# Issuing four kinds of store from GpSimd's queue in a one-core chain of attention and two feed-forward blocks

## The chip, the cores and the metric

The kernel runs on one core of one Trainium2 chip. The metric is device time in microseconds (us) of one execution. Engines are named as in the profile: PE (TensorE; PEld its weight loads), DVE (VectorE), ACT (ScalarE), POOL (GpSimd), SP (SyncE, which here only issues DMAs).

## The reference, cut to what matters

```python
# attention: 4 batches, 8 heads, 576 positions, 64 wide; heads 0-3 local mask, heads 4-7 strided mask
attn = softmax(where(mask, q @ k.T / 8, -1e9)) @ v      # -> x: 2304 tokens x 512
a = x @ w1                                              # 512 -> 1024
b = x @ w2                                              # 512 -> 1024
h = a * b @ w3                                          # 1024 -> 1024
y = h @ w_out                                           # 1024 -> 512
h = y @ w_in                                            # 512 -> 2048
g = h * sigmoid(1.702 * h)
out = g @ w_out2                                        # 2048 -> 512
```

## The kernel before

All products run in float32r with each operand split into a high and a low part; three matmuls (high*low, low*high, high*high) make one product. ACT makes the high part (L221) and DVE the low part (L227). `w3 @ w_out` is folded into one matrix first (L768), so the first block is `y = (a*b) @ wf`. Weights come in as 8-byte raw words; `to_f32` (L236 and L237 on ACT, L238 to L240 on DVE) turns them into float32 before the split.

The kernel has these stages, in order of time. An opening written out by hand (to about 45 us, `tc.manual_schedule`). Then for each of the 4 batches of 576 tokens, in halves of 288 columns: `g1` makes `a` and `b` for one of 8 row blocks m (12 matmuls each, L635), ACT copies `a` out of PSUM (L661) into a tile `abf`, and DVE multiplies `b` into it (L663). For batches 0 and 1 the product `a*b` goes out to DRAM (`abdram`, L667) and comes back later (`back`, L673); for batches 2 and 3 it is split at once into `ab`. `g2` multiplies by the folded matrix in two runs of 12 matmuls (L684); ACT copies the result into `ysb` (L690) and it is stored to `ydram` (L692). In between, `u_conv(0)` to `u_conv(7)` convert the second block's `w_in`, form the sums of a Strassen-like scheme and store them to `widram` (L946); `u_conv(8)` to `u_conv(15)` convert `w_out2` and store its parts to `wodram` (L948). From about 455 us the second block runs: `w_fetch` loads factors back from `widram` (L1006), `wt_fetch` parts from `wodram` (L1042), `quad` and `o_group` multiply (L1071, L1117), and `put` stores the output (L1131).

Tiles come from pools with a fixed number of buffers: `abf` 3, `ysb` 2, PSUM tiles `mm` 4. In the conversion of `w_out2` there are two raw tiles, one for even and one for odd numbers, and one tile `x` in two halves, so `u_conv(i + 2)` writes the half that the store of part i must have read. Parts are fetched back into the even raw tile alone, so part n + 1 is fetched when the low split of part n is done.

The text calls the eight steps `u_conv(8)` to `u_conv(15)` conversions 8 to 15, and the four parts that are split ahead of the second block parts 0 to 3 (their tiles are `w_66`, `w_68`, `w_70` and `w_72` in the listings below). The last half of batch 3 has eight `g1` groups, numbered 1 to 8 here, and four `g2` groups; `ab` of group 8 is needed by the last 3 of the 24 matmuls of the first `g2` group.

The source gives the order of recording (`weave` mixes lists by marks between 0 and 1). Outside the opening, a list scheduler then orders each engine's instructions by modelled durations, so an edit of one queue can change the order on every engine. Each engine works its list in order, and an instruction that waits holds up everything behind it; SP's list of DMA issues too.

Of the kernel before, what the change touches and what calls it, by code (L numbers as in the profile page):

```python
# [39 lines left out]
HB = S // 2  # L40
# [4 lines left out]
CW2 = 1024  # L45
# [4 lines left out]
NU = 8  # L50
# [138 lines left out]
def body(ctx: ExitStack, tc, qk, vv, mask, ql, vl, qs, vs, qmask, w1, w2, w3t, wo, win, wout, out):  # L189
    nc = tc.nc  # L190
# [20 lines left out]
    ydram = dram.tile([KC, P, NT], F32, name="ydram")  # L211
    abdram = dram.tile([4, MC, P, HB], F32, name="abdram")
    widram = dram.tile([NU, P, 7 * 256], F32, name="widram")
    wodram = dram.tile([NU, P, CW2], F32, name="wodram")
# [18 lines left out]
    def to_f32(xf, raw, n):  # L233
        rf, ri, ru = (raw.bitcast(t).rearrange("p (n t) -> p n t", t=2)[:, :n] for t in (F32, I32, U32))
        x = xf.bitcast(I32)
        nc.scalar.activation(xf, rf[:, :, 1], AF.Copy, scale=REBIAS)  # L236
        nc.scalar.activation(ri[:, :, 0], ru[:, :, 0], AF.Copy, scale=LOW)  # L237
        nc.vector.tensor_scalar(x, x, 3, BODY, op0=ALU.logical_shift_left, op1=ALU.bitwise_and)  # L238
        nc.vector.scalar_tensor_tensor(x, ri[:, :, 1], SIGN, x, op0=ALU.bitwise_and, op1=ALU.bitwise_or)  # L239
        nc.vector.tensor_tensor(x, x, ri[:, :, 0], op=ALU.add)  # L240
# [389 lines left out]
    def first(xh, cols, m, which, ps):  # L630
        ws = (w1u, w2u)[which]
        for k in range(KC):
            at = m % 2 * CW + k * P
            for a, c in ORDER:
                nc.tensor.matmul(  # L635
                    ps, ws[a][m // 2][:, at:at + P], xh[c][:, k, cols],
                    start=(k == 0 and (a, c) == ORDER[0]), stop=(k == KC - 1 and (a, c) == ORDER[-1]),
                )
# [5 lines left out]
    def new_ab(hb, m, hold, f):  # L644
        ab = abs_[m // 4][:, m % 4]
        split_ab(ab, f)
        hold[hb, m] = ab

    def g1(b, hb, m, hold, away=None):

        cols = slice(hb * HB, (hb + 1) * HB)
        st = {}

        def one(which):
            if which == 0:
                st[0] = p1.tile([P, HB], F32, tag="abf", name="abf", bufs=3)
            f = st[0]
            ps = mm.tile([P, HB], F32, tag="mm", name="ps")
            first(xt[b], cols, m, which, ps)
            if which == 0:  # L660
                nc.scalar.activation(f, ps, AF.Copy)  # L661
            else:
                nc.vector.tensor_tensor(f, ps, f, op=ALU.mult)  # L663
                if away is None:
                    new_ab(hb, m, hold, f)
                else:
                    nc.sync.dma_start(abdram[away, m], f)  # L667

        return [lambda: one(0), lambda: one(1)]

# [5 lines left out]
    def g2(b, hb, n, hold):  # L676
        st = {}

        def one(half):
            if half == 0:  # L680
                st[0] = mm.tile([P, HB], F32, tag="mm", name="ps")
            for k in range(4 * half, 4 * half + 4):
                for a, c in ORDER:
                    nc.tensor.matmul(  # L684
                        st[0], wfs[a][k][:, n * P:(n + 1) * P], hold[hb, k][:, c],
                        start=(k == 0 and (a, c) == ORDER[0]), stop=(k == MC - 1 and (a, c) == ORDER[-1]),
                    )
            if half == 1:
                ysb = p1.tile([P, HB], F32, tag="ysb", name="ysb", bufs=2)
                nc.scalar.activation(ysb, st[0], AF.Copy)  # L690
                c0 = b * S + hb * HB
                nc.sync.dma_start(ydram[n, :, c0:c0 + HB], ysb)  # L692

        return [lambda: one(0), lambda: one(1)]

# [104 lines left out]
    def half_step(k, i, h):  # L800
# [11 lines left out]
            x, x, 3, BODY, op0=ALU.logical_shift_left, op1=ALU.bitwise_and  # L812
# [108 lines left out]
    def u_load(i):  # L921

        if i >= 2 * NU:
            return
        raw = cv[i % len(cv)].tile([P, CW2], I64, tag="raw", name="raw", bufs=2 if len(cv) == 1 else 1)
        nc.sync.dma_start(raw, win[i] if i < NU else wout[i - NU])
        todo[i] = raw

    def u_conv(i, last=False):
        raw = todo.pop(i)  # L930
        if i < NU:
            x = cv[0].tile([P, 2 * CW2], F32, tag="x", name="x")
        else:
            if i == NU:
                todo["x"] = cv[0].tile([P, 2 * CW2], F32, tag="x", name="x")
            x = todo["x"][:, i % 2 * CW2:(i % 2 + 1) * CW2]
        to_f32(x[:, :CW2], raw, CW2)
        if not last:
            u_load(i + 2)
        if i < NU:  # L940
            a21, a11, a12, a22, s1, s2, s3, s4 = (x[:, n * 256:(n + 1) * 256] for n in range(8))
            nc.vector.tensor_tensor(s1, a21, a22, op=ALU.add)
            nc.vector.tensor_tensor(s2, s1, a11, op=ALU.subtract)
            nc.vector.tensor_tensor(s3, a11, a21, op=ALU.subtract)
            nc.vector.tensor_tensor(s4, a12, s2, op=ALU.subtract)
            nc.sync.dma_start(widram[i], x[:, 256:])  # L946
        else:
            nc.sync.dma_start(wodram[i - NU], x[:, :CW2])  # L948

    def u_convs(lo, hi, ahead=True):  # L950
        return [lambda i=i: u_conv(i, not ahead and i + 2 >= hi) for i in range(lo, hi)]
# [246 lines left out]
```

## Time and profile before

| | before |
|---|---|
| median of 3 runs | 841.48 us (840.9 to 843.92) |
| the profiled execution | 841.14 us |
| its span, first to last instruction | 839.3 us |
| PE busy | 804.8 us (96%) |
| DVE busy | 570.6 us (68%) |
| ACT busy | 424.4 us (51%) |
| POOL busy | 5.8 us (1%) |
| DMA moved | 117.70 MB, mean 140 GB/s |
| mean granted PE clock | 0.998 |

The profiled execution lies 1.8 us above its span and 0.3 us below the median. PE is busy nearly throughout after the first 40 us, so time is lost or won only where PE waits.

### The profile page before, as it was taken

What the parts mean: (1) busy time and instruction counts of PE and PEld (TensorE: products, weight loads), DVE (VectorE), ACT (ScalarE), POOL (GpSimd) and SP (SyncE); (2) the same over time, 40 slices, a digit from 0 to 9 for tenths busy, and PEclk for the clock granted to TensorE, in tenths of its full rate; (3) what the DMA queues carried; (4) which work ended last, traced back from release to release, by engine and by line L of the source; (5) the groups of instructions that cost most, each with busy time, mean ns of one, the idle gap of its engine ahead of it and who ended that gap; (6) DMA issues with size and microseconds to landing.
All of it is one profiled execution on the core that took longest, in us unless ns stands there. A gap on an engine that the chain in (4) does not pass through costs nothing.

```text
span 839.3 us, 15033 instructions
## 1 busy us (share of the span) xinstructions
PE 804.8 (96%) x5882; PEld 731.3 (87%) x5882; DVE 570.6 (68%) x1244; ACT 424.4 (51%) x900; POOL 5.8 (1%) x14
## 2 busy tenths in 40 slices
PE   3798999999999999999989999999999999999998
PEld 2688999977989999999989899988999988999986
DVE  3789595289776787657564988863877863877730
ACT  4788664267664564445443655542445442445330
POOL 2000000000000000000000000000000000000000
PEclk9999999999999999999999999999999999999999
DMA  9588364235676553142875441232221232212011
GB/s 344 210 307 287 108 192 137 80 123 160 241 244 207 197 201 116 51 146 103 296 234 173 143 165 59 86 113 82 87 70 64 89 113 82 89 56 77 1 38 37
DMA packets 40999, 117.70 MB, mean 140 GB/s; under 512 B 4576, under 2 KB 22496, under 8 KB 37600
## 3 DMA queue, kind: packets, MB, share of 16 engines
q1 hardware_dynamic: 40784, 116.70, 40.4%
q8 instruction: 46, 0.75, 0.4%
q14 instruction: 25, 0.20, 0.1%
q10 hardware_dynamic: 144, 0.04, 0.0%
HBM read 91.04 MB, written 25.69 MB: 139 GB/s over the span
## 4 chain that ended last, share of the span: by engine, by line
PE 79%; DMA 6%; DVE 6%; ACT 5%; issue 3%; SPq 0%; ACTq 0%; DVEq 0%
PE acc L1117 24%; PE ps L1071 20%; PE ps L635 19%; PE ps L684 9%; PE acc L768 2%; DMA wodram<-x 2%; PE sc L531 1%; PE pv L589 1%; DMA raw<-in_wout 1%; DMA abf<-abdram 1%; DMA raw<-in_w 1%; ACT xw L236 1%; ACT w L221 1%; DVE x L239 1%; DVE w L227 1%
## 5 line engine op out<-in xcount | busy, mean ns | idle before, releaser
L1117 PE MATMUL acc<-w,w 128*128 128x512 f32 x864 | 209.3, 397 | 0.0
L1117 PEld LDWEIGHTS acc<-w,w 128*128 128x128 f32 x864 | 161.7, 188 | 36.4 <-ACT w L221 0.6
L1071 PE MATMUL ps<-yq,hl 128*128 128x384 f32 x1008 | 184.2, 337 | 1.0 <-DVE hl L227 0.7
L1071 PEld LDWEIGHTS ps<-yq,hl 128*128 128x128 f32 x1008 | 177.7, 188 | 5.4 <-DVE hl L227 1.0
L684 PE MATMUL ps<-ab,w 128*128 128x288 f32 x768 | 111.2, 302 | 4.8 <-ACT abf L661 2.8
L684 PEld LDWEIGHTS ps<-ab,w 128*128 128x128 f32 x768 | 104.9, 191 | 8.5 <-DVE ab L227 3.3
L635 PE MATMUL ps<-xbh,w 128*128 128x288 f32 x512 | 102.6, 295 | 0.0
L635 PE MATMUL ps<-xah,w 128*128 128x288 f32 x512 | 102.1, 295 | 0.0
L635 PEld LDWEIGHTS ps<-xbh,w 128*128 128x128 f32 x512 | 82.1, 188 | 0.0
L635 PEld LDWEIGHTS ps<-xah,w 128*128 128x128 f32 x512 | 82.1, 188 | 0.0
L635 PE MATMUL ps<-xbl,w 128*128 128x288 f32 x256 | 78.6, 308 | 0.8 <-ACT w L221 0.7
L1062 ACT ACTIVATE sg<-c 128x384 f32<-128x384 f32 x48 | 25.0, 524 | 102.9 <-DVE c L1077 102.8
L635 PE MATMUL ps<-xal,w 128*128 128x288 f32 x256 | 76.3, 298 | 0.0
L1077 DVE TENSOR_TENSOR u<-ps,u 128x384 f32<-128x384 f32 x96 | 53.2, 554 | 10.9 <-PE ps L1071 8.9
L227 DVE TENSOR_TENSOR hl<-x,hl 128x1792 fp32r<-128x1792 f32 x24 | 48.6, 2025 | 14.0 <-ACT hl L221 14.0
L663 DVE TENSOR_TENSOR abf<-ps,abf 128x288 f32<-128x288 f32 x64 | 28.9, 453 | 33.4 <-PE ps L635 21.0
L635 PEld LDWEIGHTS ps<-xbl,w 128*128 128x128 f32 x256 | 48.0, 188 | 3.9 <-ACT w L221 0.9
L227 DVE TENSOR_TENSOR w<-gr,w 128x384 fp32r<-128x384 f32 x48 | 26.4, 557 | 33.5 <-ACT w L221 33.5
L221 ACT ACTIVATE ab<-abf 128x288 fp32r<-128x288 f32 x64 | 27.5, 441 | 42.5 <-DVE abf L663 35.7
L635 PEld LDWEIGHTS ps<-xal,w 128*128 128x128 f32 x256 | 48.1, 188 | 0.9 <-issue 0.2
L768 PE MATMUL acc<-w,w 128*128 128x512 f32 x192 | 48.0, 402 | 0.9 <-ACT w L221 0.7
L221 ACT ACTIVATE w<-gr 128x384 fp32r<-128x384 f32 x48 | 24.9, 523 | 40.6 <-PE acc L1117 40.6
(142 smaller groups left out, 1021.2 us busy)
## 6 DMA issues: line engine op xcount, KB each, us to landing
x<-widram SPq DMA_DIRECT2D x24, 896.0 KB, 4.5
raw<-in_win SPq DMA_DIRECT2D x8, 1024.0 KB, 5.6
raw<-in_wout SPq DMA_DIRECT2D x8, 1024.0 KB, 6.7
widram<-x SPq DMA_DIRECT2D x8, 896.0 KB, 5.0
raw<-in_w3t SPq DMA_DIRECT2D x10, 512.0 KB, 4.1
abdram<-abf SPq DMA_DIRECT2D x32, 144.0 KB, 2.1
abf<-abdram SPq DMA_DIRECT2D x32, 144.0 KB, 3.3
ydram<-ysb SPq DMA_DIRECT2D x32, 144.0 KB, 2.4
```

Of the source, the lines that this page charges most:

```text
L221: nc.scalar.activation(hi, src, AF.Copy)
L227: e.tensor_tensor(lo, src, r(hi), op=ALU.subtract)
L236: nc.scalar.activation(xf, rf[:, :, 1], AF.Copy, scale=REBIAS)
L239: nc.vector.scalar_tensor_tensor(x, ri[:, :, 1], SIGN, x, op0=ALU.bitwise_and, op1=ALU.bitwise_or)
L635: nc.tensor.matmul(ps, ws[a][m // 2][:, at:at + P], xh[c][:, k, cols], start=(k == 0 and (a, c) == ORDER[0]), stop=(k == KC - 1 and (a, c) ...
L663: nc.vector.tensor_tensor(f, ps, f, op=ALU.mult)
L684: nc.tensor.matmul(st[0], wfs[a][k][:, n * P:(n + 1) * P], hold[hb, k][:, c], start=(k == 0 and (a, c) == ORDER[0]), stop=(k == MC - 1 and ...
L768: nc.tensor.matmul(acc[f], hl[:, a, f * P:(f + 1) * P], wor[c][g], start=(g == 0 and (a, c) == ORDER[0]), stop=(g == MC - 1 and (a, c) == ...
L1062: nc.scalar.activation(sg, src, AF.Sigmoid, scale=1.702)
L1071: nc.tensor.matmul(ps, w[:, a, f * 256 + kk * P:f * 256 + (kk + 1) * P], yq[:, b, kk, c], start=(kk == 0 and (a, c) == ORDER[0]), stop=(kk ...
L1077: nc.vector.tensor_tensor(dst, x, y, op=ALU.add)
L1117: nc.tensor.matmul(acc[t], g[:, a, t * P:(t + 1) * P], wt[i][:, c, half], start=(i == half == 0 and (a, c) == ORDER[0]), stop=(i == NU - 1 ...
```

## The change

The DMAs of four kinds of store move from SP's queue to POOL's: `a*b` to `abdram` (32 DMAs), `y` to `ydram` (32), the `w_in` factors to `widram` (8) and the `w_out2` parts to `wodram` (8). All loads, and the output's 18 stores, stay on SP.

```diff
@@ g1
                 if away is None:
                     new_ab(hb, m, hold, f)
                 else:
-                    nc.sync.dma_start(abdram[away, m], f)
+                    nc.gpsimd.dma_start(abdram[away, m], f)
@@ g2
                 ysb = p1.tile([P, HB], F32, tag="ysb", name="ysb", bufs=2)
                 nc.scalar.activation(ysb, st[0], AF.Copy)
                 c0 = b * S + hb * HB
-                nc.sync.dma_start(ydram[n, :, c0:c0 + HB], ysb)
+                nc.gpsimd.dma_start(ydram[n, :, c0:c0 + HB], ysb)
@@ u_conv
-            nc.sync.dma_start(widram[i], x[:, 256:])
+            nc.gpsimd.dma_start(widram[i], x[:, 256:])
         else:
-            nc.sync.dma_start(wodram[i - NU], x[:, :CW2])
+            nc.gpsimd.dma_start(wodram[i - NU], x[:, :CW2])
```

The first place is SP's list behind the opening, in the listing's form with - for before and + for now; the rows L749 load raw words of `w1` and `w2`.

```order
 L297 DMA qs<-in_qs 128x1168
-L667 DMA abdram<-abf 128x288 x2
 L309 DMA vst_112<-in_vs 128x1024
 L874 DMA msk<-in_mask 128x512
 L749 DMA raw<-in_w 128x1024 x3
-L667 DMA abdram<-abf 128x288
 L294 DMA ql<-in_ql 128x896
```

The first two stores of `a*b` stood ahead of those loads and are gone from the list.

The second place is DVE's list from conversion 12 on, among the last eight `g1` groups; this is the piece of before.

```order
-L227 TENSOR_TENSOR ab_2621<-abf,ab_2621 128x288
-L663 TENSOR_TENSOR abf<-ps,abf 128x288
-L238 TENSOR_SCALAR x<-x 128x1024
-L227 TENSOR_TENSOR ab_2621<-abf,ab_2621 128x288
-L239 SCALAR_TENSOR_TENSOR x<-raw,x 128x1024
-L240 ISA x<-raw,x 128x2048
-L663 TENSOR_TENSOR abf<-ps,abf 128x288
```

And this is the piece that stands there now.

```order
+L238 TENSOR_SCALAR x<-x 128x1024
+L239 SCALAR_TENSOR_TENSOR x<-raw,x 128x1024
+L227 TENSOR_TENSOR ab_2621<-abf,ab_2621 128x288
+L240 ISA x<-raw,x 128x2048
+L238 TENSOR_SCALAR x<-x 128x1024
+L663 TENSOR_TENSOR abf<-ps,abf 128x288
+L239 SCALAR_TENSOR_TENSOR x<-raw,x 128x1024
```

Before, the product of group 2 (the first L663) stood ahead of conversion 12; now it stands behind all of 12 and the first step of 13.

The third place is ACT's list behind conversion 15, where `ab_2622` are the high splits of groups 6 to 8 and `w_66` and `w_68` those of parts 0 and 1.

```order
 L661 ACTIVATE abf<-ps 128x288
 L221 ACTIVATE w_66<-raw 128x1024
 L221 ACTIVATE ab_2622<-abf 128x288
-L690 ACTIVATE ysb<-ps 128x288
+L661 ACTIVATE abf<-ps 128x288
+L221 ACTIVATE ab_2622<-abf 128x288
+L661 ACTIVATE abf<-ps 128x288
 L221 ACTIVATE w_68<-raw 128x1024
+L221 ACTIVATE ab_2622<-abf 128x288
+L690 ACTIVATE ysb<-ps 128x288
```

Before, the split of group 8 (the first `ab_2622` row) followed part 0 alone; now part 0 stands two groups earlier, behind group 6, and the split of group 8 follows part 1. Inside a conversion the two ACT steps have also changed places: before, L237 (in place on the raw tile) came ahead of L236 (which writes the half of `x`); now L236 comes first.

## Rows read from the trace of the kernel before

**Rows 1.** Busy time by stage: us, each engine's busy us (instructions), clock, DMA share, GB/s.

```profile
90.00:390.00 300.00, 298.37 (x2232) 272.82 (x2232) 209.09 (x601) 164.87 (x437) 0.78 (x2) 1.00 0.48 159
390.00:465.00 75.00, 69.92 (x491) 68.58 (x490) 44.05 (x58) 35.81 (x54) 0.00 (x0) 0.98 0.60 198
```

**Rows 2.** Waits of SP's queue: total us, times, longest us.

```profile
SPq L667 <- DVE abf L663: 72.8, 23, 22.2
```

**Rows 3.** Timeline behind the opening: SP, DVE, ACT, PE; start us, us, instruction, [idle before].

```profile
43.34 1.53 SPq L667 DMA_DIRECT2D abdram<-abf  x2
45.93 3.31 SPq L749 DMA_DIRECT2D raw<-in_w  x3
...
38.38 0.68 DVE L817 CUSTOM_DVE_ANT_0 xw<-raw,xw 128x1024 uint16<-128x1024 uint16 x1
40.87 0.69 DVE L817 CUSTOM_DVE_ANT_0 xw<-raw,xw 128x1024 uint16<-128x1024 uint16 x1
56.30 0.69 DVE L238 TENSOR_SCALAR xw<-xw 128x1024 int32<-128x1024 int32 x1 [2.33 <-ACT xw L236]
...
53.08 1.15 ACT L237 ACTIVATE raw<-raw 128x1024 int32<-128x1024 uint32 x1 [1.77 <-DMA raw<-in_w]
...
55.62 0.92 PE L436 MATMUL pvq<-psl,vl 128*64 128x64 f32 x24 [0.79 <-ACT psl L412]
57.26 0.53 PE L635 MATMUL ps<-xbl,w 128*128 128x288 f32 x2 [0.72 <-ACT w L221]
```

**Rows 4.** Timeline of PE and DVE from the last conversion on.

```profile
438.96 5.38 PE L684 MATMUL ps<-ab,w 128*128 128x288 f32 x27 [2.83 <-ACT abf L661]
445.35 9.46 PE L684 MATMUL ps<-ab,w 128*128 128x288 f32 x69 [1.02 <-DVE ab L227]
...
442.20 1.23 DVE L240 CUSTOM_DVE_ANT_0 x<-raw,x 128x2048 uint16<-128x2048 uint16 x1
443.71 1.22 DVE L227 TENSOR_TENSOR w<-raw,w 128x1024 fp32r<-128x1024 f32 x1
444.84 0.45 DVE L227 TENSOR_TENSOR ab<-abf,ab 128x288 fp32r<-128x288 f32 x1
```

**Rows 5.** Timeline of SP and ACT over the same stretch.

```profile
428.14 0.33 SPq L926 DMA_DIRECT2D raw<-in_wout  x1
444.95 0.32 SPq L1042 DMA_DIRECT2D raw<-wodram  x1
...
437.51 1.10 ACT L237 ACTIVATE raw<-raw 128x1024 int32<-128x1024 uint32 x1 [3.19 <-DMA raw<-in_wout]
438.80 1.13 ACT L236 ACTIVATE x<-raw 128x1024 f32<-128x1024 f32 x1
448.57 1.06 ACT L221 ACTIVATE w<-raw 128x1024 fp32r<-128x1024 f32 x1 [2.11 <-DMA raw<-wodram]
458.78 0.49 ACT L1089 ACTIVATE c<-ps 128x384 f32<-128x384 f32 x1 [1.87 <-DMA ydram<-ysb]
```

**Rows 6.** The chain that ended last, one piece: start us, us, what.

```profile
414.25 8.94 DMA wodram<-x
```

**Rows 7.** Busy time in stretches of 2 us; columns as in rows 1.

```profile
436.00:438.00 2.00, 0.12 (x1) 0.00 (x0) 0.00 (x0) 0.49 (x1) 0.00 (x0) 1.00 0.99 344
442.00:444.00 2.00, 2.00 (x11) 2.00 (x10) 1.97 (x4) 0.52 (x2) 0.00 (x0) 0.54 0.00 0
```

**Rows 8.** DMA issues on SP's queue: times, KB each, median us to landing.

```profile
raw<-in_wout SPq DMA_DIRECT2D x8, 1024.0 KB, 6.7
...
ydram<-ysb SPq DMA_DIRECT2D x32, 144.0 KB, 2.4
...
wodram<-x SPq DMA_DIRECT2D x8, 512.0 KB, 5.9
```

**Rows 9.** POOL's instructions by shape: total busy us, mean ns of one.

```profile
L784 POOL MEMSET pss<- 128x1152 f32 x2 | 2.1, 1058 | 0.0
```

## The prediction

> **What bounds the kernel now.** I read busy time by stage first. PE is busy 298.37 of 300 us between 90 and 390; between 390 and 465 it has a gap of 5.1 us in 75, and there the DMA engines' mean share is 0.60 [rows 1]. The kernel is PE's, so an edit that moves only DMA issues can win no more than PE's few waits, and it can lose wherever it makes a new one. Then I read SP's queue: it stood 72.8 us in front of stores of a*b that waited for DVE [rows 2]. That looks like much, but a queue's wait matters only if a load behind it could have started and somebody waited for that load. So the third view is the timeline at the two places where PE waits on converted weights: behind the opening [rows 3] and at the end of batch 3 [rows 4, 5]. The reader is to see in the second that PE idles twice, 2.83 us up to 438.96 and 1.02 us up to 445.35, that the second wait is for the low split of group 8, and that the splits and conversion 15 on ACT and DVE, in list order, stand just ahead of it.
>
> **Opening: a gain.** Two stores of a*b held SP from 43.34 on, and the loads of raw weights behind them went out at 45.93 [rows 3]. Their raw tiles were free earlier: DVE's last readers (L817) end at 38.38 + 0.68 = 39.06 and 40.87 + 0.69 = 41.56. With the stores gone from SP's list the first two loads start 6.9 and some 4.4 us earlier. ACT waited 1.77 us for one of them at 53.08, DVE 2.33 us behind that, PE 0.79 + 0.72 = 1.51 us behind both [rows 3]. Bounds: nothing, if the next instruction in ACT's list waits for something else, and 2.33 us, DVE's whole idle. I take PE's own waits, -1.5 us.
>
> **Middle: nothing.** 90 to 390 us has most of the moved stores, but PE has little to win there: 300 - 298.37 = 1.6 us in all [rows 1]. The lists around the g2 groups are shuffled there. I take 0, with a gain of 1.6 as one bound; the loss is the second rival's.
>
> **End of batch 3: a loss, by the new order.** Call T the end of DVE's last conversion step; before, T = 442.20 + 1.23 = 443.43, and PE went on at 445.35, 1.9 us behind it, after the product of group 8, the low split of part 0 (1.22) and that of group 8 (0.45) [rows 4]. From there 9.46 us of matmuls were left. Now the high split of group 8 stands behind part 1 on ACT, and part 1 can't be fetched until the low split of part 0 has read the one raw tile. So behind T come: the product of group 6, taken as 0.45 like a split of the same 128x288 tile [rows 4]; the low split of part 0, 1.22; the fetch of part 1, 448.57 - 444.95 = 3.6; its high split, 1.06 [rows 5]; its low split on DVE, 1.22, which stands ahead of the low split of group 8; that split, 0.45. Together 8.0 us, against 1.9: PE's last wait would end 6.1 us later if T stayed.
>
> T itself moves. Conversion 15's load went out at 428.14 and landed at 437.51, 9.4 us, where the median of such loads is 6.7 [rows 5, 8]. Then ACT did L237 and, 1.3 us after that began, L236, for which DVE's first step waits. Now L236 comes first, which brings T 1.3 us forward. A load of median length would bring it 2.7 us more. I take half of that: T 1.3 + 1.35 = 2.65 us earlier. The ends are 4.0 us earlier, and 0.8 us later, if the stores that free the halves of x land later by POOL's price (next part) in two conversions, 2.1 - 1.3. The term is 6.1 - 2.65 = +3.45 us, from +2.1 to +6.9.
>
> The other shift, product 2 behind conversion 13 on DVE, makes PE stall earlier, at its fourth group. I cost it at nothing: it moves the wait of 2.83 us forward, and what covers it is the later wait for group 8, which PE meets in either case. Without that cover it would cost the whole stall.
>
> PE's clock is a further term. In 442 to 444 the granted clock was 0.54, near the lower of its two levels (1.2 of 2.4 GHz), after PE had idled nearly all of 436 to 438 [rows 7]. Before, this slow stretch ended ahead of the wait that ended at 445.35, and cost nothing. Now PE will idle some 3 us directly ahead of the last three and a bit groups. If the clock falls as it did, about 4 us at 0.54 cost 4 x 0.46 = 1.8 us. I take half, +0.9.
>
> **Price of a store on POOL.** No row shows a DMA issued by POOL. The nearest below is SP's own: the same landing, 2.4 us for ydram and 5.9 for wodram [rows 8], so 0 more. The nearest above is POOL's slowest instruction, 1.06 us [rows 9]. I take 0.5 for one store on the path. One such store is on the path: at 458.78 ACT waited 1.87 us for the last ydram store, because the second block's first tile takes that memory [rows 5]. That adds +0.5. For the wodram stores I take 0, since POOL has nothing else to issue; their range is in T. Everywhere else the buffers cover it: two ysb tiles, filled once per g2 group of some 3.2 us (9.46 us for three groups, rows 4), turn round in 6.4 us and hold a store of 2.4.
>
> A rule of the Trainium skill speaks against the change as a cure for bandwidth: "DMA: Bandwidth & Descriptors", section "Issuing engines are not separate DMA queues", says that DMAs of every issuing engine run on the same 16 engines, and that a second issuer saves only issue time. By it, conversion 15's load gains nothing from the move; with T only 1.3 us earlier the sum would be 1.35 us higher.
>
> **Sum.** -1.5 + 0 + 3.45 + 0.9 + 0.5 = +3.35 us on the profiled execution's 841.14, 844.5; that execution lies 0.3 below the median of the runs, so I forecast 844.8. The forecast's own range is from -2.3 - 1.6 + 2.1 = -1.8 to +6.9 + 1.8 + 1.06 = +9.8, or 839.7 to 851.
>
> **Rivals.** First, faster: with stores off SP's queue the loads shorten and T comes much earlier. The chain shows conversion 13 held by a store that took 8.94 us [rows 6]; if it and the load of conversion 15 took their medians, 5.9 and 6.7, T would gain 3.0 + 2.7 + 1.3 = 7.0 us. PE's last wait would then end 0.9 us earlier than before, with no slow clock, and with 2.3 from the opening the time is about 838.3; a shorter load of conversion 13 on top would give 836. The point where it decides is T earlier than 443.43 - 6.1 = 437.3. Against it: the DMA engines were at 0.99 in 436 to 438 [rows 7], so the bytes and not the queue may set the pace.
>
> Second, slower: POOL's stores land late. If a store costs POOL's 1.06 us and also waits out one DVE instruction of 1.22 [rows 4, 9], 2.3 us, then the halves of x come free 2.3 us late in conversions 11 and 13, T is 4.6 - 1.3 = 3.3 us later, the term is 9.4, and the last ydram store adds 2.3: -1.5 + 9.4 + 0.9 + 2.3 = +11.1, 852.5. It decides once a store lands over 1 us later than SP's did. The traces so far show POOL nearly unused, 0.78 us of 300 [rows 1], which tells neither way. The Trainium skill has this mechanism: "SBUF — State Buffer", section "SBUF: two separate sides", says that a DMA issued from POOL can't have its descriptors written while DVE runs an instruction that takes the shared port pair, and gives about 620 ns alone against 3100 ns overlapped. By that page's figures, an estimate of 2.5 us for each such store, the time would be close to the 852.5. No run here shows it yet.
>
> Third, the change does nothing that counts: the loads were waiting for their own tiles and not for stores, and the late split of group 8 is covered by T moving 5 to 6 us: 840.5 to 842.5.
>
> **How the numbers follow.** Forecast 0.50, faster rival 0.17, slower rival 0.18, no effect 0.15. A measurement of this kernel can tell about 0.5% from no change, 4.2 us: under 837.3 is faster, over 845.7 slower. The first rival gives 0.12 of faster, and a stray 0.01 of the forecast; slower is the second rival's 0.18 and 0.18 of the forecast, whose upper part lies over 845.7; the rest, 0.51, is within. The 8-in-10 range reaches from the middle of the faster rival, 838.3, to just under the slower one, 851.
>
> **What the new profile would show.** Right in the opening: the raw<-in_w loads issued near 39 and 41.6 and ACT's 1.77 us idle gone. Right at the end: ACT's split of group 8 waiting behind a fetch raw<-wodram, PE's last L684 wait ending near 449, slow clock behind it. The price of a store: landing of ydram within 1 us of 2.4. The prediction is wrong if T comes before 437, if stores land several us later, or if PE shows a new gap between 90 and 390, where the lists were shuffled and I followed no chain.

## The result: 1.4% slower, and the profile after

Over four runs each (the three of before and one more), the median went from 842.06 to 855.22 us: a ratio of 1.0139 (95% interval 1.0108 to 1.017). The forecast was 844.8 with a range of 838.3 to 851, so the time lies outside it, on the slow side. The profiled execution took 853.77 us, with a span of 851.7, 12.4 us longer than before; it is the shortest of the four.

PE is still the bound. The page's first part gives each engine's busy time, share and instructions.

```profile
PE 807.5 (95%) x5882; PEld 733.7 (86%) x5882; DVE 571.3 (67%) x1244; ACT 424.3 (50%) x900; POOL 51.3 (6%) x94
```

PE's work is about the same as before, so most of the 12.4 us are waits and a slower clock. To place them, the span is cut at six starts on PE that every kernel here has. These are the cuts of before that the prediction's rows don't hold: the first `g2` run, the `g1` behind the `g2` runs of that stretch, the `g1` of the last half of batch 3, and the second block (PE's timeline: start us, us, instruction).

```profile
215.05 1.76 PE L684 MATMUL ps<-ab,w 128*128 128x288 f32 x12
277.41 0.40 PE L635 MATMUL ps<-xbl,w 128*128 128x288 f32 x1
410.36 0.30 PE L635 MATMUL ps<-xal,w 128*128 128x288 f32 x1
454.65 4.35 PE L1071 MATMUL ps<-yq,hl 128*128 128x384 f32 x24
```

The same cuts of after.

```profile
217.10 1.76 PE L684 MATMUL ps<-ab,w 128*128 128x288 f32 x12
...
282.58 0.40 PE L635 MATMUL ps<-xbl,w 128*128 128x288 f32 x1
...
415.88 0.30 PE L635 MATMUL ps<-xal,w 128*128 128x288 f32 x1
...
465.94 4.35 PE L1071 MATMUL ps<-yq,hl 128*128 128x384 f32 x24
```

The first cut is PE's first L635, at 37.03 before and 38.69 after. Each stage's length is the difference of two starts; F is what is left of the span.

| stage | before | after | change | forecast |
|---|---|---|---|---|
| A: up to the first `g1` | 37.03 | 38.69 | +1.66 | 0 |
| B: up to the first `g2` | 178.02 | 178.41 | +0.39 | -1.5 |
| C: up to the `g1` behind the first `g2` stretch | 62.36 | 65.48 | +3.12 | 0 |
| D: up to the last half of batch 3 | 132.95 | 133.30 | +0.35 | 0 |
| E: up to the second block | 44.29 | 50.06 | +5.77 | +4.35 |
| F: second block | 384.65 | 385.76 | +1.11 | +0.5 |
| sum | 839.3 | 851.7 | +12.40 | +3.35 |

PE's waits after (total us, times, longest us) name the instruction that ended each.

```profile
PE ps L684 <- DVE ab L227: 7.5, 5, 3.4
...
PE ps L635 <- DVE abf L663: 3.6, 2, 3.3
```

Five waits for low splits of `ab` (L227) make 7.5 us; three of them, 4.0 us, lie in stage C. The 3.3 us for a product (L663) are the stall at the fourth `g1` group of the last half of batch 3. The view of stretches after, columns as in [rows 1], shows where PE is short.

```profile
90.00:390.00 300.00, 293.76 (x2245) 268.26 (x2245) 208.50 (x600) 162.67 (x433) 31.00 (x56) 1.00 0.46 154
390.00:465.00 75.00, 67.24 (x475) 66.06 (x474) 40.99 (x56) 33.70 (x52) 8.43 (x15) 0.95 0.63 217
456.00:458.00 2.00, 2.00 (x11) 2.00 (x10) 0.00 (x0) 0.00 (x0) 0.38 (x1) 0.50 0.44 170
```

In the 300 us of the middle PE's gaps grew from 1.63 [rows 1] to 6.24 us. At the end of batch 3 the mean clock fell from 0.98 to 0.95.

**The opening after** (timelines of SP, ACT and PE; the bracket is the idle time ahead and what ended it).

```profile
40.78 10.13 SPq L749 DMA_DIRECT2D raw<-in_w  x3
...
52.85 1.16 ACT L237 ACTIVATE raw<-raw 128x1024 int32<-128x1024 uint32 x1
...
28.90 1.55 PE L436 MATMUL pvs<-psl,lent 128*64 128x64 f32 x24 [1.07 <-ACT psl L412]
...
58.00 0.92 PE L436 MATMUL pvq<-psl,vl 128*64 128x64 f32 x24 [1.51 <-ACT abf L661]
```

The loads went out at 40.78 instead of 45.93, and ACT's idle ahead of L237 is gone [rows 3]. PE's 1.51 us of waiting is not gone: it now stands ahead of one product, for another instruction, ACT's copy of `a` (L661).

**The first `g2` stretch after.** The prediction called this the middle. One of its new waits, followed through ACT, DVE and PE.

```profile
248.32 1.13 ACT L236 ACTIVATE x<-raw 128x1024 f32<-128x1024 f32 x1 [0.65 <-DMA widram<-x]
...
249.57 1.14 ACT L237 ACTIVATE raw<-raw 128x1024 int32<-128x1024 uint32 x1
...
250.88 1.12 ACT L221 ACTIVATE ab<-abf 128x288 fp32r<-128x288 f32 x3
...
251.50 1.22 DVE L239 SCALAR_TENSOR_TENSOR x<-raw,x 128x1024 int32<-128x1024 int32 x1
252.65 1.19 DVE L227 TENSOR_TENSOR ab<-abf,ab 128x288 fp32r<-128x288 f32 x3
...
253.15 2.94 PE L684 MATMUL ps<-ab,w 128*128 128x288 f32 x20 [1.43 <-DVE ab L227]
...
268.87 2.79 PE L684 MATMUL ps<-ab,w 128*128 128x288 f32 x19 [1.71 <-DVE ab L227]
```

Three high splits of `ab` stand on ACT's list behind a conversion step that waits for a store to `widram`, and their low splits stand on DVE's list behind that conversion's next steps. They come too late for PE by 1.43 us. The wait of 1.71 us at 268.87 is of the same kind, behind an L236 that waited 1.06 us.

**The end of batch 3 after**, answering [rows 4, 5].

```profile
448.00 2.96 PE L684 MATMUL ps<-ab,w 128*128 128x288 f32 x21
454.31 11.79 PE L684 MATMUL ps<-ab,w 128*128 128x288 f32 x75 [3.35 <-DVE ab L227]
...
471.65 3.59 PE L1071 MATMUL ps<-yq,hl 128*128 128x384 f32 x19 [1.36 <-ACT c L1089]
...
444.65 1.22 DVE L240 CUSTOM_DVE_ANT_0 x<-raw,x 128x2048 uint16<-128x2048 uint16 x1
446.15 1.22 DVE L227 TENSOR_TENSOR w<-raw,w 128x1024 fp32r<-128x1024 f32 x1
452.66 1.23 DVE L227 TENSOR_TENSOR w<-raw,w 128x1024 fp32r<-128x1024 f32 x1 [3.22 <-ACT w L221]
453.81 0.45 DVE L227 TENSOR_TENSOR ab<-abf,ab 128x288 fp32r<-128x288 f32 x1
...
441.22 1.16 ACT L236 ACTIVATE x<-raw 128x1024 f32<-128x1024 f32 x1 [3.18 <-DMA wodram<-x]
...
451.57 1.06 ACT L221 ACTIVATE w<-raw 128x1024 fp32r<-128x1024 f32 x1 [2.69 <-DMA raw<-wodram]
471.11 0.49 ACT L1089 ACTIVATE c<-ps 128x384 f32<-128x384 f32 x1 [4.51 <-DMA ydram<-ysb]
...
467.00 0.54 POOL L692 DMA_DIRECT2D ydram<-ysb  x1 [2.65 <-ACT ysb L690]
```

This is the chain that the prediction described. Conversion 15 starts on ACT at 441.22, when a store to `wodram` has let its half of `x` go. DVE ends it at 444.65 + 1.22 = 445.87; then come the low split of part 0, the fetch of part 1 (ACT waits 2.69 us for `raw<-wodram`), its two splits and last the low split of group 8, and PE stands 3.35 us for it. Behind the wait lie 75 matmuls; among the first of them the granted clock falls to 0.50 (456 to 458).

**Price of a store.** DMA issues after (times, KB each, median us to landing).

```profile
ydram<-ysb POOLq DMA_DIRECT2D x32, 144.0 KB, 3.0
...
wodram<-x POOLq DMA_DIRECT2D x8, 512.0 KB, 6.8
```

The `ydram` store takes 3.0 us in the median against 2.4 [rows 8], where the trace of before tells the landing of 13 of the 32. Ahead of that, a store of `y` goes out 0.40 us behind the end of its copy on POOL and 0.03 us on SP (medians of the 32). The `wodram` store takes 6.8 against 5.9, but also 6.7 and 6.8 in two runs below that keep it on SP (lists_of_after, end_short), so no price shows there.

### The profile page after: what moved, and what is told of

The parts are those of the page before. It is cut to its first block, busy times and chain, and to the rows that moved or that the text cites. A ratio compares the mean times of both kernels' runs of the same rounds, so it can differ in the third digit from the quotient of the medians.

```text
span 851.7 us, 15099 instructions
## 1 busy us (share of the span) xinstructions
PE 807.5 (95%) x5882; PEld 733.7 (86%) x5882; DVE 571.3 (67%) x1244; ACT 424.3 (50%) x900; POOL 51.3 (6%) x94
## 4 chain that ended last, share of the span: by engine, by line
PE 66%; issue 22%; DVE 3%; DMA 3%; ACT 3%; POOL 2%; POOLq 0%; DVEq 0%; ACTq 0%; SPq 0%
PE acc L1117 24%; PE ps L1071 20%; PE ps L635 14%; PE ps L684 4%; DMA widram<-x 1%; POOL ydram L692 1%; PE sc L531 1%; PE pv L589 1%; POOL wodram L948 1%; POOL abdram L667 0%; DMA ydram<-ysb 0%; DVE hl L227 0%; PE sc L345 0%; DMA lent<-in_ql 0%; PE sc L335 0%
## 5 line engine op out<-in xcount | busy, mean ns | idle before, releaser
L635 PE MATMUL ps<-xah,w 128*128 128x288 f32 x512 | 103.5, 297 | 0.0
L635 PE MATMUL ps<-xbh,w 128*128 128x288 f32 x512 | 102.6, 295 | 0.0
L635 PEld LDWEIGHTS ps<-xah,w 128*128 128x128 f32 x512 | 83.2, 190 | 0.0
L635 PEld LDWEIGHTS ps<-xbh,w 128*128 128x128 f32 x512 | 82.1, 188 | 0.0
L635 PE MATMUL ps<-xal,w 128*128 128x288 f32 x256 | 77.3, 302 | 4.2 <-DVE abf L663 3.6
L635 PE MATMUL ps<-xbl,w 128*128 128x288 f32 x256 | 78.6, 308 | 0.1
L227 DVE TENSOR_TENSOR hl<-x,hl 128x1792 fp32r<-128x1792 f32 x24 | 48.6, 2025 | 14.2 <-ACT hl L221 14.2
L635 PEld LDWEIGHTS ps<-xal,w 128*128 128x128 f32 x256 | 48.7, 190 | 5.9 <-DVE abf L663 4.0
L635 PEld LDWEIGHTS ps<-xbl,w 128*128 128x128 f32 x256 | 48.0, 188 | 3.1 <-DVE xbl L227 0.4
L227 DVE TENSOR_TENSOR w<-gr,w 128x384 fp32r<-128x384 f32 x48 | 26.4, 557 | 33.5 <-ACT w L221 33.5
L663 DVE TENSOR_TENSOR abf<-ps,abf 128x288 f32<-128x288 f32 x64 | 29.0, 453 | 27.8 <-PE ps L635 22.6
```

Source lines behind the costliest of these rows:

```text
L227: e.tensor_tensor(lo, src, r(hi), op=ALU.subtract)
L635: nc.tensor.matmul(ps, ws[a][m // 2][:, at:at + P], xh[c][:, k, cols], start=(k == 0 and (a, c) == ORDER[0]), stop=(k == KC - 1 and (a, c) ...
```

## Experiments

Two things differ between the kernels: the queue that issues the stores, and the order in which the scheduler lays out every engine's list. The experiments take them apart. Each kernel sets the queue of the four kinds by a table `ON`. Two helpers change order alone; they add no semaphore and no work. `impose` makes each engine keep the order recorded from another build of the same source; `behind` puts one instruction behind another of the same engine.

```diff
+    for a, b in zip(names, names[1:]):            # impose: names of one engine, as recorded
+        tc.add_manual_dep(made[b], a, info, reason="recorded list")
+    for a, b in pairs:                            # behind
+        tc.add_manual_dep(made[MADE[a]], MADE[b], info, reason="list order")
```

In the diffs `POOL4` stands for all four kinds on POOL and `SP4` for all on SP. The theories: **A**, the new lists cost the time; **B**, POOL's stores are late. The table has every run's ratio to before and its stages in us (as in the table above, from its own profile).

| run | ratio [95%] | A | B | C | D | E | F |
|---|---|---|---|---|---|---|---|
| before | 1 | 37.03 | 178.02 | 62.36 | 132.95 | 44.29 | 384.65 |
| after | 1.0139 [1.0108, 1.017] | 38.69 | 178.41 | 65.48 | 133.30 | 50.06 | 385.76 |
| lists_of_before | 1.0005 [0.9978, 1.0032] | 38.49 | 177.61 | 63.62 | 133.24 | 43.98 | 385.86 |
| lists_of_after | 1.0142 [1.0081, 1.0203] | 37.01 | 180.15 | 69.77 | 133.07 | 51.39 | 383.81 |
| ab_alone | 0.9984 [0.9959, 1.0008] | 40.61 | 176.98 | 62.33 | 132.94 | 44.12 | 384.52 |
| w_in_alone | 1.0042 [1.0009, 1.0075] | 37.19 | 178.03 | 65.94 | 133.30 | 46.35 | 383.29 |
| w_out_alone | 1.0067 [1.0044, 1.0091] | 38.79 | 178.85 | 62.40 | 132.95 | 51.31 | 383.70 |
| g2_lists | 1.0121 [1.007, 1.0171] | 39.33 | 178.95 | 63.51 | 135.72 | 51.25 | 384.94 |
| end_lists | 1.0036 [1.0013, 1.0059] | 37.18 | 178.58 | 65.92 | 132.94 | 43.64 | 385.54 |
| group8_first | 1.0075 [1.0052, 1.0099] | 39.30 | 177.18 | 64.92 | 133.69 | 45.37 | 385.84 |
| vst_late | 0.9999 [0.9976, 1.0022] | 38.98 | 177.23 | 62.33 | 132.94 | 44.41 | 384.41 |
| end_short | 0.9932 [0.9908, 0.9956] | 37.23 | 180.30 | 62.36 | 132.94 | 38.41 | 386.96 |
| end_short_pool | 0.9994 [0.9978, 1.001] | 38.50 | 177.69 | 65.18 | 132.99 | 39.13 | 389.71 |

The row of before, like each other row of stages, is one execution, and before's is a short one (841.14, where its medians beside these runs were 842.76 to 843.96). So a run's rows add up to as much as 5 us more than its ratio says; B above all differs between runs with the same lists there (in the two longest, 180.15 and 180.30, the granted clock is between 0.52 and 0.63 from 58 to 62 us, and 1.00 in before). The ratio says how much, the stages where. C is steady: where its lists are those of before and the `w_in` and `y` stores are on SP, it lies between 62.33 and 62.40.

**lists_of_before: the queue without the lists.** All stores on POOL, every engine in the order of before.

```diff
+    nc = program(POOL4, lists(program(SP4), ("PE", "DVE", "Activation", "SP", "Pool")))
```

> All four kinds of stores are on POOL, and TensorE, VectorE, ScalarE and SyncE keep the order of the kernel before (SyncE's without the stores). Theory A, the new order of the lists is the loss: the new waits of PE between 215 and 282 us (4.0 us on low splits of a*b) and behind 425 us go away, a price of POOL of some 1 us for the last ydram store stays: 840 to 844 us, ratio 0.998 to 1.003. Theory B, stores land later when POOL issues them, and the queue on POOL is the loss: the time stays at 850 to 856 us, ratio 1.010 to 1.017.

Measured: 844.01 against 843.96 us. In this order the move by itself costs nothing that the ratio can tell; E comes back to that of before, and C to within 1.3 us. Its end of batch 3 shows one price of POOL (timelines of SP, POOL, ACT).

```profile
457.92 0.32 SPq L1042 DMA_DIRECT2D raw<-wodram  x1
...
458.00 0.54 POOL L692 DMA_DIRECT2D ydram<-ysb  x1 [2.65 <-ACT ysb L690]
...
462.09 0.49 ACT L1089 ACTIVATE c<-ps 128x384 f32<-128x384 f32 x1 [4.49 <-DMA ydram<-ysb]
```

ACT waited 4.49 us for the last store, against 1.87 [rows 5]: here the load of a part went out just ahead of it. A second price stands in C. Before, two stores of `y` went out ahead of a load of raw weights (SP's timeline of before).

```profile
257.06 0.79 SPq L692 DMA_DIRECT2D ydram<-ysb  x2
257.94 0.40 SPq L926 DMA_DIRECT2D raw<-in_win  x1
```

In lists_of_before the load goes out first, and ACT's next copy waits for one of the stores (SP, POOL, ACT).

```profile
258.19 0.33 SPq L926 DMA_DIRECT2D raw<-in_win  x1
...
258.59 1.14 POOL L692 DMA_DIRECT2D ydram<-ysb  x2 [10.52 <-ACT ysb L690]
...
264.04 0.41 ACT L690 ACTIVATE ysb<-ps 128x288 f32<-128x288 f32 x1 [3.48 <-DMA ydram<-ysb]
```

PE then stands 2.04 us for a split behind that copy, where before had no wait of over 0.4 us in C. g2_lists and end_short_pool, with the same order there and the stores on POOL, have the same wait (3.43 and 3.58 us on ACT).

**lists_of_after: the lists without the queue.** All stores on SP; PE, DVE and ACT in the order of after.

```diff
+    nc = program(SP4, lists(program(POOL4), ("PE", "DVE", "Activation")))
```

> The mirror of it: all stores are on SyncE again, but TensorE, VectorE and ScalarE keep the order of the changed kernel; SyncE's own order is the one that the scheduler finds for these lists. Theory A (the order of the lists): 850 to 856 us, with PE waits of 3 us and more on low splits of a*b between 215 and 282 us, and a last wait of PE on a split of group 8 of 3 us. Theory B (stores on POOL): 840 to 844 us, like the kernel before.

Measured: 856.78 us, 1.0142, as slow as the change with no store on POOL. Its PE timeline has the two losses at the same places.

```profile
235.17 2.79 PE L684 MATMUL ps<-ab,w 128*128 128x288 f32 x19 [1.50 <-DVE ab L227]
...
459.77 11.78 PE L684 MATMUL ps<-ab,w 128*128 128x288 f32 x75 [2.12 <-DVE ab L227]
```

With the run before it this decides for A: the order makes the 1.4%, and B falls as its cause. Part of this run's 69.77 us in C is a granted clock of 0.50, in 254 to 258.

**ab_alone, w_in_alone, w_out_alone: which kind re-lays the lists.** One kind of store on POOL, the others on SP, each with the lists that the scheduler then makes.

```diff
+    nc = program(dict(ab="gpsimd", y="sync", wi="sync", wo="sync"))   # ab_alone
+    nc = program(dict(ab="sync", y="sync", wi="gpsimd", wo="sync"))   # w_in_alone
+    nc = program(dict(ab="sync", y="sync", wi="sync", wo="gpsimd"))   # w_out_alone
```

> Only the 32 stores of a*b are on POOL. PE's list is that of before but for one pair of rows in the opening. Theory A: 840 to 843.5 us, no measurable difference; the wait of 1.51 us of PE near 56 us may go. Theory B: 32 of 80 stores are late, but most of them are read a hundred us later, so only the opening could lose: 841 to 845. If the slow matmuls of L436 at 29 to 33 us (1.55 and 1.43 us for 24, against 0.92) come from the change in SyncE's opening list (vst<-in_vs at 27 us), they show here too, and the time is some 1.6 us longer.

> Only the 8 stores of w_in factors are on POOL. PE's list changes at the same place as in the changed kernel, in the groups of g2 from 215 us on. Theory A: the waits of PE on low splits of a*b between 215 and 282 us are back, 3 to 4 us: 844 to 847 us. Theory B: 8 stores of 80, with readers that wait for 7 us in all in the changed kernel against 4.3 before on ScalarE, none of it on PE: 841 to 843 us.

> Only the 8 stores of w_out parts on POOL. The lists change only from the last groups of batch 2 on, and there as in the changed kernel (ScalarE's L236 ahead of L237, group 8 behind part 1). Theory A: the end stage takes 49 to 51 us against 44.3, and the rest is that of before: ratio 1.006 to 1.010, the larger part of the changed kernel's loss, from a tenth of its moved stores. Rival (the loss at the end needs the later start of the whole queue, or the ydram stores on POOL): 1.000 to 1.004.

Measured: 842.78, 846.66 and 849.54 us. The stores of `a*b`, which held SP for 72.8 us before [rows 2], are worth nothing either way. With the `w_in` stores comes the loss in C: 3.6 us more than before. E is 2.1 us longer too, though PE, DVE and ACT keep the order of before there: 69 matmuls behind the last wait take 10.99 us in place of 9.46 [rows 4], with a granted clock of 0.50 in 452 to 454. A stage can differ by that much through the clock alone.

With the `w_out` stores comes the loss at the end of batch 3, 7.0 us more in E, with PE's late wait in the same shape as after.

```profile
452.67 11.78 PE L684 MATMUL ps<-ab,w 128*128 128x288 f32 x75 [3.16 <-DVE ab L227]
```

**g2_lists and end_lists: one place at a time.** All stores on POOL; the order of before is imposed in the first `g2` stretch only (from ACT's copy of the first `y` to a copy of `a` in batch 2), or at the end of batch 3 only.

```diff
+    nc = program(POOL4, lists(program(SP4), ("PE", "DVE", "Activation", "SP"), ("y", 0, 0, 0), ("abf", 2, 0, 1)))
+    nc = program(POOL4, lists(program(SP4), ("PE", "DVE", "Activation", "SP"), ("abf", 3, 1, 0), ("y", 3, 1, 3)))
```

> All stores on POOL as in the changed kernel, but TensorE, VectorE, ScalarE and SyncE keep the order of before from the first group of g2 to the first of batch 2 (215 to 282 us); the end of batch 3 keeps the order of the changed kernel. Theory A (the order of the lists, place by place): the stretch from the first matmul of g2 to the next L635 falls from 65.5 us to about 63.6, as with all lists of before; the end of batch 3 stays long (about 50 us from the first L635 behind the earlier g2 groups to L1071). Ratio to before 1.010 to 1.013. Rival: the end alone decides, or the places are not independent: 1.013 to 1.017.

> The other half: all stores on POOL, the order of before only at the end of batch 3 (from its second half's first group to the fourth copy of y), the groups of g2 in the order of the changed kernel. Theory A: the end stage falls from 50.1 us to about 44 and the g2 stretch stays at 65.5: ratio 1.005 to 1.008, so that the two gains add up to what all lists of before give. Rival (the stores of w_out parts on POOL are what makes the end long): 1.012 to 1.016.

Measured: 1.0121 and 1.0036, the second under the 1.005 to 1.008 that were expected. C comes back to 63.51 in the first, E to 43.64 in the second, and in both the other stage stays slow. Against after's 1.0139 the first place gives back 0.0018 and the second 0.0103, together 0.0121, where both at once (lists_of_before) give 0.0134. The first figure is smaller than its interval can tell. It is also no clean price: behind the imposed stretch DVE's and ACT's lists are those of neither kernel, and D takes 135.72 us there, 2.4 more than in after. The first place's price rests on stage C.

**group8_first: the one order that the forecast blamed.** The kernel after, with the two splits of part 1 put behind those of group 8.

```diff
+    nc = program(POOL4)   # and, inside:
+    behind(tc, (("part hi", 1), "ab hi"), (("part lo", 1), "ab lo"))
```

> The changed kernel with two list edges at the end of batch 3: the high split of group 8 ahead of the high split of part 1 of w_out on ScalarE, the low split of group 8 ahead of the low split of part 1 on VectorE. If the chain of the prediction holds (PE's last wait ends 8 us behind the last conversion step because group 8 stands behind the fetch of part 1), the wait of 3.35 us goes, and with it the slow stretch of TensorE behind it: 4 to 5 us less than the changed kernel, ratio to before 1.007 to 1.010. Rival: another wait takes its place (the fetch or the second block's first group): 1.012 to 1.016.

Measured: 848.42 us, 1.0075. The last wait is gone: PE does the 96 matmuls of the last `g2` in one stretch and E falls from 50.06 to 45.37; PE's stall at the fourth group, 3.28 us, is still there.

```profile
447.66 12.96 PE L684 MATMUL ps<-ab,w 128*128 128x288 f32 x96
```

**vst_late: stage A.** In after, 24 matmuls near 29 us took 1.55 us instead of 0.92. The theory was that a load of `vst`, which goes out earlier once `a*b`'s stores have left SP, disturbs them. The kernel is ab_alone with that load behind two loads of raw weights.

```diff
+    nc = program(dict(ab="gpsimd", y="sync", wi="sync", wo="sync"))   # and, inside:
+    behind(tc, (("vst", 6), ("raw", 6)), ("msk", ("vst", 6)))
```

> Only the stores of a*b on POOL, and on SyncE's list the loads vst<-in_vs and msk stand behind the first two of the three raw loads of the opening, where no store holds them: they go out at some 43 us and not at 27. If the load of vst at 27 us is what makes the 24 matmuls of L436 at 28.9 and 31.3 us take 1.55 and 1.55 us in place of 0.92, they take 0.92 again, and the time is 1.2 to 1.6 us less than with the stores of a*b alone: ratio to before 0.995 to 0.998. Rival (the issue on POOL itself, or TensorE's clock by chance): the matmuls stay at 1.55 and the ratio at 0.997 to 1.001.

Measured: the load went out late, and the matmuls were as slow (SP's and PE's timelines). The theory falls; the rival named there, TensorE's clock, is taken up in the last section.

```profile
44.02 0.38 SPq L309 DMA_DIRECT2D vst<-in_vs  x1
...
29.18 1.55 PE L436 MATMUL pvs<-psl,lent 128*64 128x64 f32 x24 [1.07 <-ACT psl L412]
```

**end_short: a better order.** If order is what counts there, the kernel before can gain from it too. Its stores stay on SP; conversion 15's first steps are put behind the splits of group 8, and part 2 behind the first copy of the second block.

```diff
+    nc = program(SP4)   # and, inside:
+    behind(tc, (("high", 15), "ab hi"), (("low", 15), "ab hi"), (("shift", 15), "ab lo"),
+           (("part hi", 2), ("c", 0)))
```

> The kernel before, stores on SyncE, with four list edges at the end of batch 3: conversion 15 stands behind the splits of group 8 on ScalarE and VectorE, and the split of part 2 of w_out stands behind the second block's first copy L1089. If the order of these few rows is what PE waits for there, its waits (2.8 and 1.0 us in the trace of before) and the slow stretch of some 1.7 us behind the first go: 4 to 5 us less, ratio 0.994 to 0.9955; with a new wait for the last ydram store 0.996 to 0.998. Rival: conversion 15 and the parts of w_out, now later, are what PE waits for next: 0.999 to 1.002.

Measured: 838.58 against 843.65 us, 0.9932 [0.9908, 0.9956], faster than both kernels and a little under the range expected. PE's timeline shows no wait up to the second block, and then a longer one.

```profile
438.44 12.96 PE L684 MATMUL ps<-ab,w 128*128 128x288 f32 x96
...
457.50 2.87 PE L1071 MATMUL ps<-yq,hl 128*128 128x384 f32 x8 [1.91 <-ACT c L1089]
```

E is 5.9 us shorter than before's, F 2.3 longer.

**end_short_pool: the same lists, stores on POOL.**

```diff
+    nc = program(POOL4, lists(program(SP4), ("PE", "DVE", "Activation", "SP")))   # recorded from end_short
```

> The same lists on TensorE, VectorE and ScalarE, and SyncE's without the stores, with all four kinds of stores on POOL. If the issuing queue is worth little once the lists are held, it stays within 0.3% of the same lists with the stores on SyncE, some 1 to 3 us slower for the last ydram store and the g2 groups as with the lists of before. Rival: with the end shortened, a queue without stores lets loads start earlier, and it is 1 to 3 us faster.

Measured: 0.9994 of before, 0.6% over end_short, with intervals that don't touch: this expectation missed. So the queue is not free in every order. By the spans of the two, POOL loses 2.8 us in C, 1.3 in A, 0.7 in E and 2.75 in F, and wins 2.6 in B, 5.0 in all; but A and B differ by as much through the clock between kernels with the same lists there (the note under the table, the last section). In C stands the wait of lists_of_before, and the 12 matmuls behind it take 3.04 us against 1.87 there, at a granted clock of 0.50 in 266 to 268. F is seen in its timelines.

```profile
453.98 0.32 SPq L1042 DMA_DIRECT2D raw<-wodram  x1
...
454.55 0.54 POOL L692 DMA_DIRECT2D ydram<-ysb  x1 [0.60 <-ACT ysb L690]
...
460.99 0.49 ACT L1089 ACTIVATE c<-ps 128x384 f32<-128x384 f32 x1 [6.85 <-DMA ydram<-ysb]
```

## Why the prediction was wrong, step by step

**Middle: "The lists around the g2 groups are shuffled there. I take 0".** This is the step that failed: a term put at nothing without a chain behind it. It cost 3.12 us in C and 0.35 in D, the largest part of the 9.05 us (12.40 - 3.35) by which the stages miss the sum; the opening missed by 1.9, stage A by 1.7, the clock term by 1.4 and the last store by 0.6, all the same way. The prediction left a loss here to the second rival, as a late store; the larger part is the order. lists_of_after loses 7.4 us in C with no store on POOL, w_in_alone 3.6 with only the `widram` stores there; g2_lists and lists_of_before, with the old order and the stores on POOL, take 2.0 and 1.9 of the 3.1 us away. The 1.2 us that stay come with the stores on POOL: ACT's wait for a store that went out behind a load. The 2.8 in end_short_pool are the same wait and the slow clock behind it. The prediction had no piece of this stretch's lists before it and followed no chain there.

**Opening: -1.5.** Half of the step held: the loads went out 5 us earlier and ACT's 1.77 us of idle vanished. PE's 1.51 us did not; the product now waits for L661, on which no term was made. lists_of_before, with the opening's lists of before, has the same wait (1.48 us), so the list is not its cause. In all eight kernels with the stores of `a*b` on POOL PE waits there for L661, 1.22 to 1.62 us, and in none of the other five. That the product is given another PSUM tile, one that L661 has to empty first, would fit; this was only argued.

**Stage A: +1.66.** The prediction had no term here. The slower matmuls near 29 us account for about 0.6 + 0.5 us of it. That is TensorE's clock, which in this execution rose some 5 us later than in that of before (last section).

**End of batch 3: +3.45.** Right in place, mechanism and size. PE's last wait ends at 454.31, in a stage that begins 415.88 - 410.36 = 5.52 us later, so at 448.79 in the time of before: 3.44 us behind 445.35. T, forecast 2.65 us earlier, came 443.43 - (445.87 - 5.52) = 3.08 earlier; the chain behind it took 8.44 us instead of 8.0; the two misses cancel, so the agreement to 0.01 us is luck. T came forward by both of the causes named: 1.3 us by the order of the two ACT steps, and 1.8 because ACT could start sooner. The load of conversion 15 went out at 434.08 and was there by 441.22, so it took at most 7.1 us against 9.4. What ACT waited for last was not that load but a store to `wodram`, issued at 434.43 and landed at 441.2. group8_first takes the wait away with two changes of order, and w_out_alone makes it without the other stores.

**The other shift, at nothing.** It held. PE's stall moved forward to 431.44 and was 3.29 us long, against 2.83, and the wait for group 8 covered it: 3.44 + 2.33 us (next paragraph) are all of E's 5.77.

**Slow clock: +0.9, measured +2.33 for all that lies behind the wait.** 75 matmuls in 11.79 us stand against 69 in 9.46. At the 12.96 / 96 = 0.135 us of group8_first, the six more cost 0.81, a term that the prediction did not have; the other 1.52 is the clock, granted at 0.50 in 456 to 458. The prediction took half of a bound of 1.8 and should have taken nearly all of it: PE's second idle of over 3 us was in its own sum.

**Last store: +0.5, measured +1.04.** PE's wait for the copy behind it grew from 0.32 to 1.36 us. The term was sized by the price of one store, and that was fair: the median rose 0.6 us. What makes it larger seems to be what went ahead. On SP the order of the list kept the load of the next part behind the last store; on two queues the load no longer waits for it. In after the load is issued 0.58 us ahead and in lists_of_before 0.08, and the store lands 4.0 us after its issue in both. In end_short_pool it is 0.57 us ahead, behind another load, and PE's wait for the copy is 3.70 us against 1.91 in end_short. In group8_first, also on POOL, the load goes out 0.59 us behind the store, and the store lands in 2.05 us. The place in C shows the same. But no run moved a load alone, and end_short's last store, on SP with that load behind it, still took 4.9 us.

**Rivals.** The second, 852.5, came nearest to the measured time, and that is luck: its +11.1 us are not there. Its condition was a store over 1 us late. The `ydram` median is 0.6 us later from the issue and another 0.4 from the copy's end, so the condition was about met, but in the order of before all of it together costs no more than 2.7 us (the interval of lists_of_before, up to 1.0032), and in that of end_short some 5. Under a busy DVE, where that rival put the delay, the longest issue of after stands in these rows (timelines of POOL and DVE).

```profile
110.46 1.81 POOL L667 DMA_DIRECT2D abdram<-abf  x1 [3.27 <-DVE st L536]
...
110.87 1.29 DVE L238 TENSOR_SCALAR xw<-xw 128x1024 int32<-128x1024 int32 x2
```

POOL's issue of a store takes some 0.54 us; here it takes 1.81 and ends 0.11 us behind the second of two L238. The Trainium skill, "SBUF — State Buffer", section "SBUF: two separate sides", gives some 3100 ns for a DMA issued from POOL that overlaps a DVE `tensor_copy`, against 620 ns alone. The trace agrees that such an issue waits for DVE, but not that it happens often: of the 80 issues in after 5 took over 0.6 us, 4 of them under an L238, 2.2 us more in all and none of them a store of `y`, though DVE was busy for 67% of the span. The first rival (faster) fell: T came at 440.35 and not before 437.3. The third fell with the end of batch 3. The Trainium skill, "DMA: Bandwidth & Descriptors", section "Issuing engines are not separate DMA queues", says that DMAs of every issuer run on the same 16 engines and that a second issuer saves only the time of issuing. The median load of `w_out2`, 6.2 us after and 6.7 before [rows 8], and the 1.0005 agree with it.

Of the 12.40 us, then, the 5.77 in E and 1.9 of those in C go when the old order is imposed; 1.2 in C and the 1.11 in F stay with the stores on POOL; A's 1.66 is the clock; 0.7 in B and D is not placed.

## What to carry to other kernels

Where a scheduler lays out the lists, an edit of a queue is two edits: record the lists of one version and impose them on the other, and the two come apart in two runs. In a forecast, follow the chain at every place where the listing differs, at each wait that PE has little slack for; a shuffled list is not a term of zero. Two queues also lose an order that one queue kept: look for a store that somebody waits for and that a load can now overtake. Once a late operand is found, look for the order that brings it earlier: four order edges took 0.7% off the kernel before, while 72.8 us of a queue's waiting, taken away, gave nothing (ab_alone).

## What the runs showed that was not expected

A pair of 24-matmul groups (L436, near 29 and 31 us) takes 0.92 to 0.94 us each in 5 of the 13 kernels profiled and 1.43 to 1.55 in the other 8. It is TensorE's clock. In two of the 8, ab_alone and end_short_pool, the view shows the lower level there (ab_alone, columns as in [rows 1]).

```profile
28.00:30.00 2.00, 0.93 (x17) 0.84 (x18) 1.19 (x3) 1.84 (x4) 0.00 (x0) 0.50 1.01 379
```

In the other six the trace's record of the clock begins, at 1.00, only at 32.4 to 34.4 us; in the five quick kernels it begins at 27.4 to 28.3, ahead of the pair. Where nothing is recorded the view prints 1.00. So in after the clock rose behind the pair and in before ahead of it. Why it rose later stays open: up to 28.89 us PE's rows of end_lists (quick) and w_out_alone (slow) agree to 0.01 us. Of the kernels with the stores of `a*b` on POOL 7 of 8 have it (not end_lists), of the others 1 of 5 (w_out_alone), one execution each; these matmuls lie ahead of the first such store, which went out at 45.3 us in after. The one load that was tried, `vst`, is not the cause.

Orders decided here at no cost in instructions: the same stores on the same queue gave 0.9932 or 1.0142 of the time of before, by the order of the lists alone.
